# Fused forgetting attention and MoE: the first 128 tokens of all batches as groups of their own, the rest by batch, diagonal blocks in one score chunk

## The chip, the cores and the metric

The kernel runs on one NeuronCore of a Trainium2 chip. The metric is the device time of one execution in microseconds (us), as a median over several runs. In brackets after a ratio stands its 95% interval.

Engines are named as in the profile: PE is TensorE's matmul unit, PEld its weight loads, DVE is VectorE, ACT is ScalarE, POOL is GpSimd, SP is SyncE (here it only issues DMAs).

## The reference

```python
# B=8 batches, H=8 heads, S=576 tokens, D=64;  MoE: d_model 512, d_ff 2048
scores = q @ k.T / sqrt(D)
cum    = cumsum(log(clip(f, 1e-4, 1)), axis=-1)
scores = where(causal, -1e9, scores + cum[q] - cum[k])       # forgetting decay
attn   = softmax(scores);  x = attn @ v                      # (B, H, S, D)
x      = x.transpose(0, 2, 1, 3).reshape(B * S, H * D)       # 4608 x 512
h      = x @ w_in                                            # 4608 x 2048
out    = (h * sigmoid(h)) @ w_out                            # 4608 x 512
```

Attention of one batch feeds 576 rows of the MoE. Attention is small in PE work and heavy on the other engines: in the kernel before, what is not the MoE's takes 61 us of PE's busy time, but 144 us of DVE's and 127 us of ACT's. What is called the MoE here is the two matrix products of `h` and `out`: 1152 matmuls of 128x128 by 512 columns, most of PE's time (282 of 343 us busy in the kernel before). The art of the kernel is to keep PE fed with MoE matmuls while the other engines do the attention of later batches.

## The kernel before

Two heads form a pair `n`, two pairs a quad `m`; a batch has two quads. `scores` makes scaled exponents in chunks of 512 columns and masks the diagonal blocks. A quad's `dn` matmuls make the denominators and the two halves of the numerators. ACT evicts them, DVE takes reciprocals, and `divide` writes the attention output `xT`, which is the MoE's moving operand.

```python
    def scores(n, c):
        # ... matmuls of chunk c into sc; exponent of 2x512 on ACT into u ...
        if c % 2 == 0:
            return
        d = [u[:, :, UO[c - 1] : UO[c - 1] + P], u[:, :, UO[c] : UO[c] + P]]
        for x in d:                                   # four such masks per pair
            nc.vector.tensor_tensor(
                out=x, in0=x, in1=mask[:, None, :].to_broadcast([P, 2, P]), op=ALU.mult
            )
        # ... and mask_t for the last 64 columns if c == 3 ...
```

The MoE is cut into nine groups of 512 tokens. `m1_chunk` makes one 128-row slice of `h` (four W_in matmuls into `hp`, tanh on ACT, one DVE operation into `gt`), `m2_part` a quarter of one output tile (four W_out matmuls into `po`). `fill(n)` emits `n` such units between pieces of attention. The kernel fixes each engine's order itself (`manual_schedule`), and the traces show the operations in the order of emission: in `e1_fill20` below PE waits 1.40 us for a divide while matmuls that need not wait stand behind. `finished` says which groups may be emitted:

```python
    for n in range(2 * NP, NU):                       # the steady part
        b, p = divmod(n, NP)
        scores(n, 0)
        scores(n, 1)
        fill(2)
        if p == 0:
            finished(n - 1)                           # groups of the batch before: only now
        # ... loads, casts, transposes for later pairs ...
        fill(1)
        scores(n, 2)
        scores(n, 3)
        fill(3)
        if n % 2 == 1:
            m = n // 2
            fill(1)
            den(m); rec_part(m, 0)                    # (joined here)
            for e in range(2):
                num(m, e)
            fill(1)
            rec_part(m, 1)
            for e in range(2):
                divide(m, e, nc.gpsimd)
            fill(2)
```

The softmax here doesn't subtract the row's maximum and nothing guards it: scores larger than these inputs give would overflow.

Of the kernel before, what the change touches and what calls it, by code (L numbers as in the profile page):

```python
# [18 lines left out]
def kernel(  # L19
# [14 lines left out]
    NT = B * S  # L34
# [4 lines left out]
    NU = B * NP  # L39
# [3 lines left out]
    NX = 2 * NM + 1  # L43
    NPT = 2 * NP
    NQ = NU // 2
    HD = D // 2
    assert D == 64 and S == 576 and DM == H * D and NP == NCC
# [6 lines left out]
    conv = ctx.enter_context(tc.tile_pool(name="conv", bufs=3))  # L54
    vpool = ctx.enter_context(tc.tile_pool(name="vpool", bufs=3))
# [5 lines left out]
    opool = ctx.enter_context(tc.tile_pool(name="opool", bufs=2))  # L61
# [4 lines left out]


# [6 lines left out]

    def load_qk(n):
        b, p = divmod(n, NP)
        ts = []
        for name, src in (("qf", q), ("kf", k)):
            t = stage.tile([P, 2 * NM * D], FP32, name=name, tag=name, bufs=4)
            for i in range(2):  # L80
                s = src[b, 2 * p + i, 0:SM, :]
                if n < NPT:
                    nc.sync.dma_start(
                        out=t[:, i * NM * D : (i + 1) * NM * D],
                        in_=s.rearrange("(p c) d -> p (c d)", p=P),
                    )
                else:
                    nc.sync.dma_start(
                        out=t[:, :].rearrange("p (c h d) -> p c h d", h=2, d=D)[:, :, i, :],
                        in_=s.rearrange("(c p) d -> p c d", p=P),  # L90
                    )
            ts.append(t)
        qst[n] = tuple(ts)
# [10 lines left out]

    def cast_qk(n, engs):
        b, p = divmod(n, NP)
        t2 = conv.tile([P, NX, 2 * D], BF16, name="qkb", tag="qkb")
        for i, t in enumerate(qst.pop(n)):
            c0 = i * (NM + 1)
            dst = t2[:, c0 : c0 + NM, :]  # L110
            if n < NPT:
                engs[i].tensor_copy(  # L112
                    out=dst.rearrange("p c (h d) -> p c h d", h=2),
                    in_=t[:, :].rearrange("p (h c d) -> p c h d", h=2, d=D),
                )
            else:
                engs[i].tensor_copy(out=dst, in_=t[:, :].rearrange("p (c x) -> p c x", c=NM))  # L117
        nc.gpsimd.tensor_copy(
            out=t2[:, NM, :],
            in_=tst[b][:, 2 * p : 2 * p + 2, :].rearrange("s h d -> s (h d)"),  # L120
        )
        qbf[n] = t2

    def load_v(b, c):
        if b not in vst:
            vst[b] = [
                stage.tile([P, H, D], FP32, name=f"vf{i}", tag=f"vf{i}") for i in range(NM + 1)
            ]
        r = slice(0, P) if c < NM else slice(ST, P)
        nc.sync.dma_start(  # L130
            out=vst[b][c][r, :, :],
            in_=v[b, :, c * P : min(S, (c + 1) * P), :].rearrange("h p d -> p h d"),
        )

    f_sb = setup.tile([BH, S], FP32, name="f_sb")
    nc.sync.dma_start(out=f_sb[:, :], in_=f.rearrange("b h s -> (b h) s"))
    load_qk(0)
    load_tails(0)
    for n in range(1, NP):
        load_qk(n)  # L140
    for c in range(NM + 1):
        load_v(0, c)


    ident_bf = const.tile([P, P], BF16, name="ident_bf")
    make_identity(nc, ident_bf)
    ident_f = const.tile([BH, BH], FP32, name="ident_f")
    make_identity(nc, ident_f)
    mask = const.tile([P, P], BF16, name="mask")
    make_upper_triangular(nc, mask, val=1.0, diag=True)  # L150
    mask_t = const.tile([P, ST], BF16, name="mask_t")
    nc.gpsimd.memset(mask_t[0:ST, :], 0.0)
    make_upper_triangular(nc, mask_t[ST:P, :], val=1.0, diag=True)

    xT = const.tile([P, NCC, NT], BF16, name="xT")
    w_in_bf = const.tile([P, NCC, DFF], BF16, name="w_in_bf")
    w_out_bf = const.tile([P, NFC, DM], BF16, name="w_out_bf")
    w_bf = const.tile([P, NM + 1, BH], BF16, name="w_bf")

# [12 lines left out]
    def load_w_out(i):  # L172
# [5 lines left out]


# [4 lines left out]
    half = setup.tile([BH, 1], FP32, name="half")  # L184
    nc.scalar.activation(out=f_sb[:, :], in_=f_sb[:, :], func=ACT.Ln)
    nc.vector.tensor_tensor_scan(  # L186
        out=cum[:, :],
        data0=f_sb[:, :],
        data1=f_sb[:, :],
        initial=0.0,  # L190
        op0=ALU.add,
        op1=ALU.bypass,
    )
    nc.vector.tensor_scalar_mul(out=half[:, :], in0=cum[:, S - 1 : S], scalar1=0.5)
    wexp = setup.tile([BH, S + ST], FP32, name="wexp")
    nc.scalar.activation(
        out=wexp[:, 0:S], in_=cum[:, :], func=ACT.Exp, bias=half[:, 0:1], scale=-1.0
    )
    cast_qk(0, (nc.vector, nc.vector))
    nc.vector.tensor_copy(out=wexp[:, S : S + ST], in_=wexp[:, SM:S])  # L200

# [7 lines left out]
    qkT: dict[int, bass.AP] = {}  # L209
    us: dict[int, tuple] = {}  # L210

    def convert_v(b, c, eng=nc.gpsimd):
        if b not in vbf:
            vbf[b] = vpool.tile([P, NM + 1, H, D], BF16, name="vp", tag="vp")
        vp = vbf[b]
        r = slice(0, P)
        if c == NM:
            r = slice(ST, P)
            eng.memset(vp[0:ST, NM, :, :], 0.0)
        n = r.stop - r.start  # L220
        eng.tensor_tensor(  # L221
            out=vp[r, c, :, :],
            in0=vst[b][c][r, :, :],
            in1=w_bf[r, c, b * H : (b + 1) * H, None].to_broadcast([n, H, D]),
            op=ALU.mult,
        )


    def k_off(kb):
        return SM if kb == NM else S + ST + kb * P  # L230

    def transposes(n, evac=nc.vector.tensor_copy):
        src = qbf.pop(n)
        t = qktp.tile([P, NX, P], BF16, name="qkT", tag="qkT")
        qkT[n] = t[:, :, :].rearrange("p x c -> p (x c)")
        if n >= NPT:
            nc.sync.dma_start_transpose(
                out=t[:, :, :], in_=src[:, :, :].rearrange("p x c -> p (x c)")
            )
            return  # L240
        for x0 in (0, NM + 1):
            tp = pbig.tile([P, P, NM], FP32, name="tp", tag="big")
            for c in range(NM):
                nc.tensor.matmul(  # L244
                    tp[:, :, c],
                    lhsT=src[:, x0 + c, :],
                    rhs=ident_bf[:, :],
                    start=True,
                    stop=True,
                )  # L250
            evac(  # L251
                out=t[:, x0 : x0 + NM, :].rearrange("p x c -> p (x c)"),
                in_=tp[:, :, :].rearrange("p t c -> p (t c)"),
            )
            if x0 == 0:
                tt = pbig.tile([P, 8 * P], BF16, name="tt", tag="big")
                nc.tensor.transpose(tt[:, 0:P], src[:, NM, :], ident_bf[:, :])
                evac(out=t[:, NM, :], in_=tt[:, 0:P])


    UO = [0]
    for kb in range(NM + 1):
        UO.append(UO[-1] + S - kb * P)
    UW = UO[-1]
    CB = [min(c * 512, UW) for c in range(5)]

    def scores(n, c):
        if c == 0:
            us[n] = upool.tile([P, 2, UW], BF16, name="u", tag="u")
# [3 lines left out]
        c0, c1 = CB[c], CB[c + 1]  # L273
        for kb in range(NM + 1):
            lo, hi = max(UO[kb], c0), min(UO[kb + 1], c1)
            if lo >= hi:
                continue
            q0 = kb * P + lo - UO[kb]
            for i in range(2):
                r = slice(i * D, (i + 1) * D)  # L280
                nc.tensor.matmul(  # L281
                    sc[:, i, lo - c0 : hi - c0],
                    lhsT=t[r, k_off(kb) : k_off(kb) + P],
                    rhs=t[r, q0 : q0 + hi - lo],
                    start=True,
                    stop=True,
                )
# [3 lines left out]
        if c % 2 == 0:  # L291
            return
        d = [u[:, :, UO[c - 1] : UO[c - 1] + P], u[:, :, UO[c] : UO[c] + P]]
        for x in d:
            nc.vector.tensor_tensor(  # L295
                out=x, in0=x, in1=mask[:, None, :].to_broadcast([P, 2, P]), op=ALU.mult
            )
        if c == 3:
            x = u[:, :, UO[NM] : UW]
            nc.vector.tensor_tensor(  # L300
                out=x, in0=x, in1=mask_t[:, None, :].to_broadcast([P, 2, ST]), op=ALU.mult
            )


    QS = 2 * P

    def q_parts(kb):
        if kb * P < QS:
# [284 lines left out]
```

## Time and profile before

| | before |
|---|---|
| time, median | 370.55 us (370.54 to 373.25, 3 runs; 370.98 us with a fourth, which the result below uses) |
| PE busy | 343.0 us, 93% of the span |
| PE's share of the chain that ended last | 73% |
| masks on DVE | 72.7 us in 160 operations |
| MoE alone at the end | from 296 us |

First the page's line of engine totals (busy us, share of the span, instructions), and the rows of PE and of its granted clock, in tenths over 40 equal slices:

```profile
PE 343.0 (93%) x2957; PEld 163.7 (44%) x2957; DVE 240.0 (65%) x368; ACT 233.7 (63%) x363; POOL 141.5 (38%) x195
...
PE   2669778999999999999999999999999999999995
...
PEclk9977996999999999999999999999999999999999
```

Apart from the tail in the last slice, PE loses time only in the first eight slices, 75 us. The busy time by stretches says the same (the columns are length, busy us of each engine with instructions, granted clock, DMA share, GB/s):

```profile
0.00:75.00 75.00, 54.16 (x590) 30.28 (x591) 55.94 (x96) 47.84 (x69) 42.68 (x70) 0.89 1.05 199
75.00:296.00 221.00, 218.28 (x2042) 101.56 (x2041) 159.82 (x240) 158.37 (x248) 96.07 (x124) 1.00 0.68 141
296.00:370.40 74.40, 70.61 (x328) 31.81 (x325) 24.27 (x34) 27.46 (x46) 2.75 (x2) 1.00 0.12 47
```

From 75 us on PE is busy 218 of 221 us at full clock.

```profile
PE hp L381 <- DVE qkT L251: 4.4, 3, 2.5
PE hp L381 <- POOL xT L360: 1.6, 6, 0.7
```

The divides (`POOL xT`) hold up W_in for 1.6 us in the whole run.

### The profile page before, as it was taken

How to read it: one execution, taken by the hardware profiler on the slowest of the kernel's cores; microseconds unless marked ns; L12 is line 12 of the kernel's file. 1: busy time of each engine (PE TensorE's matmuls, PEld its weight loads, DVE VectorE, ACT ScalarE, POOL GpSimd, SP SyncE). 2: the span in 40 equal slices, each digit the busy share in tenths (PEclk: the TensorE clock that was granted, in tenths of full speed). 3: DMA queues.
4: the chain of work that ended last, by engine and by line, in shares of the span. 5: the costliest groups of instructions: out<-in, count | busy, mean ns of one | idle time of the engine just before them, and what ended most of it. 6: DMA issues, size and time to landing. Idle time of an engine off the chain costs nothing.

```text
span 370.4 us, 7558 instructions
## 1 busy us (share of the span) xinstructions
PE 343.0 (93%) x2957; PEld 163.7 (44%) x2957; DVE 240.0 (65%) x368; ACT 233.7 (63%) x363; POOL 141.5 (38%) x195
## 2 busy tenths in 40 slices
PE   2669778999999999999999999999999999999995
PEld 1437342435454545454535454545354544444442
DVE  4678886897667766777777677766776626443400
ACT  4676674876868686868686867686767626344321
POOL 3796582091419150916092609260833020000000
PEclk9977996999999999999999999999999999999999
DMA  6999899999938964796569656976220010001012
GB/s 181 234 192 231 186 190 190 183 196 202 229 77 191 200 135 104 176 213 146 92 144 223 157 104 148 198 159 124 60 62 29 30 58 28 28 30 57 29 58 85
DMA packets 141299, 49.67 MB, mean 134 GB/s; under 512 B 129424, under 2 KB 135568, under 8 KB 141264
## 3 DMA queue, kind: packets, MB, share of 16 engines
q1 hardware_dynamic: 134928, 44.99, 56.7%
q0 software_dynamic: 6336, 4.21, 7.3%
q8 instruction: 23, 0.38, 0.4%
q14 instruction: 12, 0.10, 0.1%
HBM read 36.85 MB, written 9.44 MB: 125 GB/s over the span
## 4 chain that ended last, share of the span: by engine, by line
PE 73%; DVE 11%; ACT 8%; issue 3%; POOL 2%; DMA 1%; POOLq 0%; ACTq 0%
PE hp L381 31%; PE po L408 29%; DVE rec L348 7%; PE dn L331 7%; PE sc L281 6%; ACT u L288 4%; ACT rec L343 3%; POOL xT L360 2%; PE tp L244 1%; DVE qkT L251 1%; ACT th L389 1%; DVE u L295 1%; DVE xT L360 1%; DMA f_sb<-in_f_dram 1%; DVE cum L186 0%
## 5 line engine op out<-in xcount | busy, mean ns | idle before, releaser
L381 PE MATMUL hp<-xT,w_in_bf 128*128 128x512 bf16 x576 | 142.5, 385 | 7.2 <-DVE qkT L251 4.4
L408 PE MATMUL po<-w_out_bf,gt 128*128 128x512 bf16 x576 | 139.7, 380 | 0.0
L390 DVE SCALAR_TENSOR_TENSOR gt<-th,hp 128x512 bf16<-128x512 bf16 x144 | 95.7, 678 | 56.0 <-ACT th L389 55.9
L389 ACT ACTIVATE th<-hp 128x512 bf16<-128x512 f32 x144 | 85.1, 602 | 69.3 <-PE hp L381 69.2
L288 ACT ACTIVATE u<-sc 128x1024 bf16<-128x1024 f32 (+1 forms) x128 | 99.9, 838 | 16.2 <-PE sc L281 16.2
L360 POOL TENSOR_TENSOR xT<-nm,rec 128x576 bf16<-128x576 f32 x28 | 39.3, 1422 | 142.5 <-DVE rec L348 132.1
L295 DVE TENSOR_TENSOR u<-u,mask 128x256 bf16<-128x256 bf16 x128 | 62.9, 518 | 37.3 <-ACT u L288 36.9
L381 PEld LDWEIGHTS <-w_in_bf 128*128 128x128 bf16 x576 | 54.4, 99 | 72.8 <-issue 12.5
L408 PEld LDWEIGHTS <-gt 128*128 128x128 bf16 x576 | 53.4, 98 | 64.5 <-issue 2.5
L348 DVE RECIPROCAL rec<-rec 128x288 f32<-128x288 f32 x32 | 60.2, 1922 | 13.9 <-ACT rec L343 13.9
L221 POOL TENSOR_TENSOR vp<-vf,w_bf 128x512 bf16<-128x512 f32 (+1 forms) x40 | 41.5, 1053 | 2.2 <-DMA vf<-in_v_dram 1.2
L281 PE MATMUL sc<-qkT 64*128 64x64 bf16 (+4 forms) x384 | 34.9, 285 | 4.8 <-ACT u L288 2.9
L417 ACT ACTIVATE osb<-po 128x512 f32<-128x512 f32 x36 | 21.6, 600 | 20.4 <-PE po L408 20.4
L281 PEld LDWEIGHTS <-qkT 64*128 64x128 bf16 x384 | 14.2, 95 | 38.8 <-issue 29.0
L331 PE MATMUL dn<-u,vp 128*32 128x320 bf16 (+4 forms) x896 | 28.7, 270 | 1.7
L355 ACT ACTIVATE nm<-dn 128x576 f32<-128x576 f32 x32 | 20.8, 650 | 6.3 <-PE dn L331 6.0
L331 PEld LDWEIGHTS <-vp 128*32 128x32 bf16 x896 | 22.0, 100 | 6.1 <-issue 3.3
L343 ACT ACTIVATE rec<-dn 128x576 f32<-128x576 f32 x16 | 10.4, 650 | 17.8 <-PE dn L331 17.8
L244 PE MATMUL tp<-ident_bf,qkb 128*128 128x128 bf16 x64 | 11.6, 373 | 6.8 <-DVE qkb L112 6.8
L331 PE MATMUL dn<-u,w_bf 128*32 128x320 bf16 (+4 forms) x448 | 15.1, 272 | 3.0 <-ACT u L288 2.4
L117 POOL CAST qkb<-qf 128x512 bf16<-128x512 f32 x24 | 16.6, 693 | 0.0
L117 POOL CAST qkb<-kf 128x512 bf16<-128x512 f32 x24 | 15.0, 626 | 2.3 <-DMA kf<-in_k_dram 2.3
(42 smaller groups left out, 93.5 us busy)
## 6 DMA issues: line engine op xcount, KB each, us to landing
out_dram<-osb SPq DMA_DIRECT2D x36, 256.0 KB, 2.1
qf<-in_q_dram SPq DMA_DIRECT2D x64, 128.0 KB, 3.2
kf<-in_k_dram SPq DMA_DIRECT2D x64, 128.0 KB, 3.2
vf<-in_v_dram SPq DMA_DIRECT2D x32, 256.0 KB, 4.8
w_in_bf<-in_moe_w_in_dram POOLq DMA_DIRECT2D x8, 256.0 KB, 15.8
w_out_bf<-in_moe_w_out_dram POOLq DMA_DIRECT2D x4, 512.0 KB, 11.7
qktf<-in_q_dram SPq DMA_DIRECT2D x8, 128.0 KB, 3.0
qktf<-in_k_dram SPq DMA_DIRECT2D x8, 128.0 KB, 3.7
```

The costliest lines, as they stand in the source:

```text
L117: engs[i].tensor_copy(out=dst, in_=t[:, :].rearrange("p (c x) -> p c x", c=NM))
L221: eng.tensor_tensor(out=vp[r, c, :, :], in0=vst[b][c][r, :, :], in1=w_bf[r, c, b * H : (b + 1) * H, None].to_broadcast([n, H, D]), op=ALU. ...
L281: nc.tensor.matmul(sc[:, i, lo - c0 : hi - c0], lhsT=t[r, k_off(kb) : k_off(kb) + P], rhs=t[r, q0 : q0 + hi - lo], start=True, stop=True,)
L288: nc.scalar.activation(out=u[:, :, c0:c1], in_=sc[:, :, 0 : c1 - c0], func=ACT.Exp, scale=scale)
L295: nc.vector.tensor_tensor(out=x, in0=x, in1=mask[:, None, :].to_broadcast([P, 2, P]), op=ALU.mult)
L331: nc.tensor.matmul(dn[HD * j : HD * (j + 1), 512 - QS + q0 : 512 - QS + q1], lhsT=w, rhs=u_part(n, i, kb, q0, q1), start=(kb == 0), stop=( ...
L348: nc.vector.reciprocal(out=recs[qd][:, r], in_=recs[qd][:, r])
L360: eng.tensor_tensor(out=xT[:, (2 * qd % NP) + e, b * S : (b + 1) * S], in0=nms.pop((qd, e))[:, :], in1=recs[qd][:, :], op=ALU.mult,)
L381: nc.tensor.matmul(hp[:, :], lhsT=w_in_bf[:, cc, fc * P : (fc + 1) * P], rhs=xT[:, cc, t0 : t0 + TG], start=(cc == 0), stop=(cc == NCC - 1),)
L389: nc.scalar.activation(out=th[:, :], in_=hp[:, :], func=ACT.Tanh, scale=0.5)
L390: nc.vector.scalar_tensor_tensor(out=gt[:, fc, :], in0=th[:, :], scalar=1.0, in1=hp[:, :], op0=ALU.add, op1=ALU.mult,)
L408: nc.tensor.matmul(po[:, :], lhsT=gt[:, fc, tb * P : (tb + 1) * P], rhs=w_out_bf[:, fc, :], start=(fc == 0), stop=(fc == NFC - 1),)
```

## The change

The intent: start the MoE earlier, and give DVE fewer and larger mask operations. The first 128 tokens of a batch need only one diagonal block per head. So these "heads" of all eight batches are attended first, and form three groups (512, 256, 256 tokens). The rest of each batch, 384 tokens, is a group of its own; the last 64 tokens of four batches make a group of 256. In the rest's scores the diagonal blocks lie side by side in one chunk, with one mask. `fill` now takes a budget in microseconds. Cut to its core:

```diff
-    TG = 512
-    NG = NT // TG
+    GW = [4 * P, 2 * P, 2 * P] + [RB] * NM + [NM * ST] + [RB] * (B - NM) + [(B - NM) * ST]
+    # ... load_qk0, turn0 (turning by 64x64 matmuls), scores0, out0: attention of the heads ...
+    CHUNKS = [
+        [(1, 0, P, 0), (2, P, 2 * P, P), (3, 2 * P, RQ, 2 * P), (4, RB, RQ, 2 * P + P + ST)],
+        [(0, 0, RQ, SM)],
+        [(1, P, RQ, SM + RQ), (2, 2 * P, RQ, SM + RQ + 2 * P + ST)],
+    ]
-        for x in d:
-            nc.vector.tensor_tensor(
-                out=x, in0=x, in1=mask[:, None, :].to_broadcast([P, 2, P]), op=ALU.mult
-            )
+        if c == 0:
+            x = u[:, :, 0:SM]
+            nc.vector.tensor_tensor(
+                out=x, in0=x, in1=maskf[:, None, :].to_broadcast([P, 2, SM]), op=ALU.mult
+            )
+    # ... step(): W_in of the next ready group if it is no further on than W_out of the one before
+    FILL = 2.6
+    for m in range(NQ):
+        n = 2 * m
+        scores(n, 0)
+        scores(n, 1)
+        prepare(n)
+        fill(FILL)
+        scores(n, 2)
+        scores(n + 1, 0)
+        prepare(n + 1)
+        fill(FILL)
+        scores(n + 1, 1)
+        scores(n + 1, 2)
+        fill(FILL + 1.0)
+        finish_quad(m)          # dn matmuls, evictions, reciprocals
+        fill(FILL)
+        for e in range(2):
+            divide(m, e, nc.gpsimd)
+        if m % 2 == 1:
+            b = m // 2
+            ready.add(REST_OF[b])       # the batch's own group, at once
+            if b in (NM - 1, B - 1):
+                ready.add(TAILS_OF[b][0])
```

## The prediction

> **What bounds the kernel now.** The tensor engine (PE): 93% busy in the page's engine table, 73% of the chain of work that ended last. By the busy times of stretches, PE is busy 54 of the first 75 us (granted clock 0.89), 218 of 221 us in 75–296 us, and from 296 us does MoE matmuls alone, ending in a tail of some 3 us. In the timeline eight 128x512 matmuls take 1.73 us, 216 ns each[...]. My estimate of PE's work: 1152 MoE matmuls 249 us; attention 9.8 us per batch (scores 0.90 per pair, 2.5 per quad, ten switches at 0.1), 78 us; transposes 8 us: 335 us. About 35 us are lost, nearly 30 before 75 us.
>
> **What the change does** (estimates from those durations).
> - PE work: W_in matmuls become 832 (512, 256, 384 columns)[...]; rest attention 4.35 us per quad, 69 us; heads with their 64x64 turning matmuls 2.3 us per batch, 18 us. Total 337 us: no less than before.
> - Start: MoE can begin once four heads are done. DVE paces this: per batch an eviction 0.6, a mask 0.6–0.9, a reciprocal of 256 (6.4 ns per element) 1.65, a divide 0.65 us, after some 11 us (f, log, scan, exponent). First MoE matmul at 27 us (before: 36.5), then dense, with some 6 us of stalls where batches 4, 5 meet group 1. The rest starts at 80 us with 24 us lost.
> - DVE: 128 masks of 256 (518 ns mean) and 32 of 128 become 40 of 1024, saving about 35 us, off the critical path. ACT: 32 small exponents fewer, 64 more W_in evictions, about +10 us.
>
> **Where it loses.** Groups follow batches. A batch's rest gives 384 tokens x 54 ns = 20.8 us of MoE; two quads ask for 22.8. By the instruction order, no MoE work is left at the ends of quads 1, 3, 5 and 7: after the dn matmuls come ten score matmuls and then W_in matmuls of the group just attended, which wait for an evict 0.5, two reciprocals 2.95 and POOL divides about 2.5 us. PE idles nearly 4 us, four times: 15 us. The work also separates into quads with only W_in and quads with only W_out matmuls; the first load ACT to about 95%. The end of the last quad waits 2 us. After quad 8 groups overlap again and PE should be dense.
>
> **Sum.** 337 work + 24 start + 15 starvation + 2 last quad + 3 tail = 381; less 2 for doubt about the small matmuls' costs: 379 us. 8 in 10: 364 to 392 us. Chances: faster by over 2% 0.12, within 2% 0.40, slower 0.48.
>
> **What would show each step.** First hp matmul at 25–30 us, rest scores from 75–85 us; four waits of hp for POOL's divide, 3–4 us each, some 33 us apart, between 105 and 215 us; hp of 384 columns in runs of six chunks; the mask group at 0.7–0.9 us x40; dense PE afterwards; the MoE-only end about 33 us rather than 74.
>
> **What would make it wrong.** Divides landing sooner than their chain suggests, so no starvation (then about 363). A start sooner than 27 us. Weights landing late (second W_in half after 34 us), which would stall the early MoE and add 5–10 us. [...] ACT, not PE, limiting the W_in-only quads.

The sum came to 381 us, 379 us after the 2 us for doubt. The 0.6 us for 256 additional W_in matmuls is contained in the 337 us of work (249 + 69 + 18 = 336 without it). The 6.4 ns per element can be read from DVE's timeline of the kernel before: two reciprocals of 288 elements start at 106.10 us, and the next operation at 109.78, 3.68 us later.

## More of the kernel before

A verdict is "unclear" when the interval reaches over the mark of 2%.

From the groups of instructions (busy us, mean ns of one, idle before), the two kinds of MoE matmul and the masks, and from the list of waits (total us, times, longest) what W_in matmuls waited for:

```profile
L381 PE MATMUL hp<-xT,w_in_bf 128*128 128x512 bf16 x576 | 142.5, 385 | 7.2 <-DVE qkT L251 4.4
L408 PE MATMUL po<-w_out_bf,gt 128*128 128x512 bf16 x576 | 139.7, 380 | 0.0
...
L295 DVE TENSOR_TENSOR u<-u,mask 128x256 bf16<-128x256 bf16 x128 | 62.9, 518 | 37.3 <-ACT u L288 36.9
```

## The result, and the profile after

The changed kernel takes 404.25 us (403.94 to 404.49, 4 runs) against 370.98 us (370.54 to 373.25). The ratio is 1.087, with a 95% interval of 1.0832 to 1.0908. A ratio here is worked out by the program that took the times, over the runs of the same rounds, so it is not quite the ratio of the medians. The span of the profiled run is 402.4 us, 32.0 us more than before.

The same views as before. The engine totals, with the rows of PE and of the clock:

```profile
PE 349.2 (87%) x3682; PEld 192.7 (48%) x3717; DVE 208.6 (52%) x310; ACT 235.7 (59%) x408; POOL 151.7 (38%) x252
...
PE   3639799899879959996995999999799989979995
...
PEclk9958999999969999996999899999899989999999
```

The holes are no longer at the start alone: there is one about every 3.5 slices, and the clock dips next to most of them. The busy time by stretches (columns as before):

```profile
0.00:80.00 80.00, 58.64 (x718) 35.98 (x725) 50.98 (x71) 34.84 (x58) 38.75 (x69) 0.91 0.94 166
80.00:359.00 279.00, 252.00 (x2748) 134.94 (x2771) 142.07 (x207) 183.57 (x313) 112.95 (x183) 0.95 0.55 118
359.00:402.40 43.40, 38.51 (x221) 21.73 (x223) 15.53 (x32) 17.31 (x39) 0.00 (x0) 0.99 0.13 43
```

In the middle stretch PE is idle 27 of 279 us and has a mean clock of 0.95. The groups, and the waits of W_in:

```profile
L504 PE MATMUL po<-w_out_bf,gt 128*128 128x512 bf16 x544 | 135.1, 381 | 3.0 <-issue 1.0 <-ACT osb L513 0.6 <-PE dn L429 0.2
L478 PE MATMUL hp<-x,w_in_bf 128*128 128x384 bf16 x512 | 105.7, 350 | 21.6 <-POOL x L460 20.5 <-DVE gt L487 0.8
...
L410 DVE TENSOR_TENSOR u<-u,maskf 128x1024 bf16<-128x1024 bf16 x32 | 27.1, 846 | 36.5 <-ACT u L405 36.4
```

```profile
PE hp L478 <- POOL x L460: 20.5, 14, 2.7
PE hp L478 <- DVE x L321: 4.9, 2, 4.0
PE hp L478 <- DVE gt L487: 3.5, 4, 2.5
```

The masks of the rest take 27.1 us, and those of the heads 6.9 us more, where all masks took 72.7 us before. The wait of W_in for the divides rose from 1.6 to 20.5 us. (The counts of matmuls are a little short, as some records are missing from a trace.) One such wait in PE's timeline, at the end of quad 1 (start, us, line, operation, count, and in brackets the idle time before it):

```profile
107.03 0.61 PE L429 MATMUL dn<-u,vp 128*32 128x128 bf16 x24
108.10 0.40 PE L398 MATMUL sc<-qkT 64*128 64x128 bf16 x8 [0.46 <-ACT nm L447]
108.54 0.37 PE L398 MATMUL sc<-qkT,kT 64*128 64x448 bf16 x2
108.84 0.50 PE L478 MATMUL hp<-x,w_in_bf 128*128 128x384 bf16 x2
112.06 0.48 PE L478 MATMUL hp<-x,w_in_bf 128*128 128x384 bf16 x1 [2.72 <-POOL x L460]
113.29 4.32 PE L478 MATMUL hp<-x,w_in_bf 128*128 128x384 bf16 x13 [0.75 <-POOL x L460]
117.54 1.04 PE L398 MATMUL sc<-qkT 64*128 64x320 bf16 x12
```

After the last `dn` matmuls come the next quad's scores and then at once W_in matmuls of the group that was attended just before. The first two read the parts of `x` that quad 0 had written; the third waits for quad 1's divides. Then 13 matmuls of 384 columns take 4.32 us, where 16 take 2.77 us elsewhere. The chain they waited for, in DVE's and POOL's timelines of the same time:

```profile
107.65 2.97 DVE L452 RECIPROCAL rec<-rec 128x224 f32<-128x224 f32 x2 [4.16 <-ACT rec L444]
```

```profile
110.79 2.73 POOL L460 TENSOR_TENSOR x<-nm,rec 128x384 bf16<-128x384 f32 x4 [3.66 <-DVE rec L452]
```

The divides end at 113.5 us, 5.9 us after the last `dn` matmul.

The waits in PE's timeline are at the ends of quads 1, 3, 5, 7, 11, 13 and 15: 3.93, 4.14, 3.98, 4.15, 2.32, 2.03 and 2.26 us of idle time (scores' waits included), 22.8 us together. The clock is at half (granted 0.5, and 1.0 elsewhere) in six stretches after 110 us, one from near the end of each of these but the last: two of 6.8 and four of 3.4 us, 27.3 us in all. PE was busy 24.4 us of that, so an estimate of what the half clock cost is 24.4 / 2 = 12.2 us. Idle time and clock together are 35 us, a little more than the whole 32.0 us of difference. In the 3.4 us before each of the six stretches, PE's records cover 0.3 to 1.4 us.

### The profile page after: what moved, and what is told of

Same layout as the page of the kernel before. It is cut to its first block, busy times and chain, and to the rows that moved or that the text cites. A ratio compares the mean times of both kernels' runs of the same rounds, so it can differ in the third digit from the quotient of the medians.

```text
span 402.4 us, 9181 instructions
## 1 busy us (share of the span) xinstructions
PE 349.2 (87%) x3682; PEld 192.7 (48%) x3717; DVE 208.6 (52%) x310; ACT 235.7 (59%) x408; POOL 151.7 (38%) x252
## 4 chain that ended last, share of the span: by engine, by line
PE 67%; DVE 9%; issue 6%; ACT 6%; DMA 5%; POOL 4%; SPq 2%; POOLq 0%; ACTq 0%
PE po L504 28%; PE hp L478 27%; PE dn L429 6%; PE sc L398 5%; DMA vf<-in_v_dram 4%; DVE rec L452 4%; POOL x L460 3%; ACT u L405 2%; DVE gt L487 2%; DVE rec L317 2%; ACT th L486 1%; ACT rec L444 1%; DMA w_in_bf<-in_moe_w_in_dram 1%; SPq L127 1%; DVE x L321 1%
## 5 line engine op out<-in xcount | busy, mean ns | idle before, releaser
L478 PE MATMUL hp<-x,w_in_bf 128*128 128x384 bf16 (+2 forms) x829 | 156.2, 332 | 30.3 <-POOL x L460 20.5
L487 DVE SCALAR_TENSOR_TENSOR gt<-th,hp 128x384 bf16<-128x384 bf16 (+2 forms) x208 | 103.0, 518 | 87.2 <-ACT th L486 84.9
L486 ACT ACTIVATE th<-hp 128x384 bf16<-128x384 f32 (+2 forms) x208 | 94.6, 473 | 80.7 <-PE hp L478 74.9
L478 PEld LDWEIGHTS <-w_in_bf 128*128 128x128 bf16 x832 | 81.9, 102 | 96.3 <-issue 52.9
L460 POOL TENSOR_TENSOR x<-nm,rec 128x384 bf16<-128x384 f32 x64 | 46.3, 754 | 171.8 <-DVE rec L452 171.8
L452 DVE RECIPROCAL rec<-rec 128x224 f32<-128x224 f32 x32 | 47.4, 1524 | 38.5 <-ACT rec L444 38.5
L410 DVE TENSOR_TENSOR u<-u,maskf 128x1024 bf16<-128x1024 bf16 x32 | 27.1, 846 | 36.5 <-ACT u L405 36.4
L398 PE MATMUL sc<-qkT 64*128 64x128 bf16 (+3 forms) x384 | 23.2, 242 | 2.0 <-ACT nm L447 2.0
L429 PE MATMUL dn<-u,vp 128*32 128x128 bf16 (+3 forms) x768 | 19.7, 237 | 0.0
L335 POOL CAST qkb<-qf 128x384 bf16<-128x384 f32 x32 | 18.4, 574 | 0.8 <-PE hp L478 0.5
```

The source lines that it names most:

```text
L335: nc.gpsimd.tensor_copy(out=t2[:, c0 : c0 + NR, :].rearrange("p c x -> p (c x)"), in_=t[:, :, :, :].rearrange("p c h d -> p (c h d)"),)
L398: nc.tensor.matmul(sc[:, i, o - c0 : o - c0 + q1 - q0], lhsT=kt, rhs=t[r, q0:q1], start=True, stop=True,)
L410: nc.vector.tensor_tensor(out=x, in0=x, in1=maskf[:, None, :].to_broadcast([P, 2, SM]), op=ALU.mult)
L429: nc.tensor.matmul(dn[HD * j : HD * (j + 1), q0:q1], lhsT=w, rhs=us[n][:, i, o : o + q1 - q0], start=(kb == 0), stop=(kb == NM),)
L452: nc.vector.reciprocal(out=recs[qd][:, r], in_=recs[qd][:, r])
L460: eng.tensor_tensor(out=xg(g)[:, cc, g0 : g0 + c1 - c0], in0=nm[:, c0:c1], in1=rec[:, c0:c1], op=ALU.mult,)
```

## The experiments

Theory 1: PE starves at the batch ends. By the order of emission it has no other MoE work there, waits for the divides, and then runs at half clock. Theory 2: PE simply has more to do (832 W_in matmuls for 576, turning matmuls, narrower pieces). Theory 3: ACT limits the new mix.

### Less MoE work asked for: `e1_fill20`

```diff
-    FILL = 2.6
+    FILL = 2.0
```

> One number changed: the MoE budget between attention pieces is 2.0 instead of 2.6 us, so that by the order of emission no quad runs out of MoE work. Theory 1 (the matrix engine starves at batch ends because two quads ask for more MoE work than one batch's rest supplies, waits for the divides, and then runs at half clock): the waits of hp for POOL's divide fall from 20 us to under 4, the half-clock stretches after 110 us vanish, and the time falls by 28 to 36 us to 368-376 us. Theory 2 (the matrix engine simply has more work: 832 instead of 576 W_in matmuls, turning matmuls, narrower attention pieces): waits move elsewhere and the time stays above 392 us. Theory 3 (ScalarE limits the new mix): shorter gaps between attention pieces load it more, so 400 us or more.

Measured: 384.22 us (381.85 to 386.5), ratio 1.0328 [1.0277, 1.0379]. That refutes theories 2 and 3 as the main cause: one number that removes no work takes 20 us away. But it misses my range by 8 us. The waits of W_in for the divides, from the list of waits, and the end of quad 1 in PE's timeline:

```profile
PE hp L478 <- POOL x L460: 10.5, 8, 1.5
```

```profile
104.50 1.67 PE L504 MATMUL po<-w_out_bf,gt 128*128 128x512 bf16 x7 [0.16 <-issue]
106.10 0.40 PE L398 MATMUL sc<-qkT 64*128 64x128 bf16 x8
106.34 0.35 PE L398 MATMUL sc<-qkT,kT 64*128 64x448 bf16 x2
106.62 0.50 PE L478 MATMUL hp<-x,w_in_bf 128*128 128x384 bf16 x2
108.52 0.32 PE L478 MATMUL hp<-x,w_in_bf 128*128 128x384 bf16 x1 [1.40 <-POOL x L460]
110.20 2.65 PE L478 MATMUL hp<-x,w_in_bf 128*128 128x384 bf16 x9 [1.35 <-POOL x L460]
```

W_out work was now left at the batch end. PE did 1.7 us of it, and still waited, because the rule that picks the next unit took W_in of the fresh group before the rest of W_out. By the order of emission 1, 4, 7 and 10 units of W_out stood behind it at the ends of quads 1, 3, 5 and 7. So "no work left" was not quite the cause. What counts is how much other work stands in PE's queue between a batch's attention and the first W_in matmul of its own group. I call this theory 1a.

### The clock by itself: `e2_warm`

```diff
+    def warm(n):                       # result never read
+        jk = pbig.tile([P, 512], FP32, name="jk", tag="big")
+        for _ in range(n):
+            nc.tensor.matmul(jk[:, :], lhsT=w_in_bf[:, 0, 0:P], rhs=w_in_bf[:, 0, 0:512], start=True, stop=True)
     ...
         prepare(n)
+        if m in (2, 4, 6, 8):
+            warm(16)
+        if m in (12, 14):
+            warm(10)
         fill(FILL)
```

> The changed kernel with its budget of 2.6 us, but with matmuls whose result nobody reads (16 of 128x512, 3.45 us, at the first MoE slot of quads 2, 4, 6, 8, and 10 of them, 2.15 us, at quads 12 and 14) filling the time in which the matrix engine would wait for the divides. No work is taken away and no wait is shortened. If the half clock after each wait is a cost of its own (theory 1, second half): the granted clock stays at 1.0 after 110 us and the time falls by 9 to 13 us, to 391-395 us. If the clock dips are only a record of idleness: 402-406 us.

Measured: 394.55 us, ratio 1.0613 [1.0589, 1.0637], 9.7 us less than the changed kernel by the medians and about as much by the two ratios (1.0613 for 1.087). The busy time by stretches (columns as before) shows a mean clock of 1.00, and PE's timeline shows the dummy matmuls (`jk`) in place of the wait and 13 W_in matmuls at full rate, 2.27 us in place of 4.32:

```profile
80.00:380.00 300.00, 288.53 (x3017) 158.44 (x3048) 156.97 (x239) 198.62 (x347) 112.90 (x183) 1.00 0.54 113
```

```profile
109.75 3.40 PE L676 MATMUL jk<-w_in_bf 128*128 128x512 bf16 x15 [0.16 <-issue]
112.99 0.65 PE L478 MATMUL hp<-x,w_in_bf 128*128 128x384 bf16 x3
113.98 2.27 PE L478 MATMUL hp<-x,w_in_bf 128*128 128x384 bf16 x13 [0.34 <-POOL x L460]
```

More work made the kernel faster. The half clock is a cost of its own, some 10 us of the 33.

### The length of the chain: `e6_divdve`

```diff
         for e in range(2):
-            divide(m, e, nc.gpsimd)
+            divide(m, e, nc.gpsimd if e == 0 else nc.vector)
```

> The changed kernel (budget 2.6, early release) with the second of each quad's two divides on VectorE instead of GpSimd, so that the two run side by side and the chain from attention to W_in is some 1.0 to 1.3 us shorter. Theory 1: each of the seven waits shrinks by about 1 us, some half-clock stretches vanish with it: 390 to 398 us. If the waits are only due to missing work and not to the length of the chain, or if VectorE's own queue eats the gain: 402 to 406 us.

Measured: 393.34 us, ratio 1.0578 [1.0515, 1.064]. W_in's wait for POOL's divides is 14.7 us in the list of waits, for 20.5. The half-clock stretches after 110 us shrank from 27.3 to 17.1 us. Shortening the chain by about 1 us at a time gave 11 us in all: 5.8 us less of waiting, and some 4 us by the same estimate for the half clock (16.1 us busy at half clock for 24.4). So the waits do follow the chain.

### Releasing the group later: `e4_late18a`, `e5_late18b`

```diff
-    FILL = 2.6
+    FILL = 1.8
+    def finished(b):
+        ready.add(REST_OF[b])
+        if b in (NM - 1, B - 1):
+            ready.add(TAILS_OF[b][0])
     ...
         fill(FILL)
+        if m > 0 and m % 2 == 0:        # e4: here; e5: after the second fill(FILL)
+            finished(m // 2 - 1)
         scores(n, 2)
     ...
-        if m % 2 == 1:
-            b = m // 2
-            ready.add(REST_OF[b])
-            if b in (NM - 1, B - 1):
-                ready.add(TAILS_OF[b][0])
+        if m == NQ - 1:
+            finished(m // 2)
```

> Budget 1.8 us, and a batch's rest group is released to the MoE only after the first MoE slot of the next quad (it was: right after its divides are issued). By the emission order no slot is empty, and 3.9 to 4.3 us of other MoE work stands between the end of a batch's attention and the first W_in matmul of its own group in the four early batches (the first run: 1.7 us; the change: 0). The divides land some 4.5 us after the attention ends, so the waits should almost close. Theory 1a (what counts is how much other work is queued ahead of a fresh group on the in-order matrix engine): hp's waits for POOL's divide under 3 us in total, no half clock after 110 us, 368 to 373 us. If the 384 us of the first run came from other costs: 380 us or more.

> As the run before it, but the group is released after the second MoE slot: 5.2 to 5.4 us of other work ahead of it in the early batches, with one slot about 1 us short at quad 2. Theory 1a: no wait for POOL's divide at all, 367 to 373 us, within 2 us of the other. If later release starves the engine instead: 3 us or more slower than the other.

Measured: 372.81 us (ratio 1.0022 [0.9961, 1.0083]) and 372.55 us (ratio 1.0022 [0.9957, 1.0087]). Both expectations of theory 1a are met, and W_in's wait for POOL's divides is all but gone from both lists of waits. The same place in PE's timeline of the first of the two:

```profile
102.30 0.62 PE L429 MATMUL dn<-u,vp 128*32 128x128 bf16 x24
102.84 2.76 PE L504 MATMUL po<-w_out_bf,gt 128*128 128x512 bf16 x12
105.54 0.40 PE L398 MATMUL sc<-qkT 64*128 64x128 bf16 x8
105.77 0.35 PE L398 MATMUL sc<-qkT,kT 64*128 64x448 bf16 x2
106.06 1.90 PE L504 MATMUL po<-w_out_bf,gt 128*128 128x512 bf16 x8
107.89 0.62 PE L398 MATMUL sc<-qkT 64*128 64x320 bf16 x12
108.44 1.47 PE L478 MATMUL hp<-x,w_in_bf 128*128 128x384 bf16 x8
```

Twenty W_out matmuls and the scores now stand between the `dn` matmuls and W_in, 5.5 us. The last divide that W_in reads ends at 108.73 us, just before the fourth W_in matmul, which reads it first, starts at 108.94. No half-clock stretch is left in this run from 33 us to the end of the matmuls; the second run has one, of 3.4 us at 49 us, still in the start. So 31 of the 33 us (some 30 by the repeat `e4_again` below) come from the budget and the order of release, two scheduling choices around an otherwise unchanged set of operations.

No run separates the two. Followed through from the code of `step` and `fill`, budget 1.8 with the early release would leave 1.7 to 2.6 us of other MoE work between attention and W_in at the ends of quads 1, 3 and 5; the late release makes that 3.9 to 4.3 us. From quad 7 on, the smaller budget alone leaves 6.7 us and more, because it puts MoE work off. So the release should matter at the first three batch ends only, but that is worked out and not measured.

### The masks: `e3_mask2`, `e10_mask2late`, `e7_diag`

The first two apply the mask of the rest's diagonal chunk twice (the values are 0 and 1, so the result is the same):

```diff
                 out=x, in0=x, in1=maskf[:, None, :].to_broadcast([P, 2, SM]), op=ALU.mult
             )
+            nc.vector.tensor_tensor(
+                out=x, in0=x, in1=maskf[:, None, :].to_broadcast([P, 2, SM]), op=ALU.mult
+            )
```

> Budget 2.0 as in the first run, and the mask of the diagonal chunk applied twice (0 and 1, so the result is the same): VectorE gets 32 more operations of about 0.85 us, 27 us in all, which is most of what the single score chunk saved it. If VectorE is off the critical path, as I predicted: within 2 us of the run with budget 2.0. If the diagonal chunk's saving counts: 8 us or more slower than that run.

> The late-release version with every mask of the rest applied twice: 27 us more of VectorE, as in the third run, but now on a kernel whose matrix engine has no waits for divides. The third run cost 6.5 us where such waits were left. If VectorE mattered there only as part of the chain that the waits follow: under 2 us slower than the base. If VectorE limits the W_in stretches by itself: 5 us or more slower.

`e3_mask2` took 390.69 us, 6.5 us more than the run with budget 2.0. It had four half-clock stretches after 80 us where the other had two. That lies between the two outcomes written down (within 2 us, or 8 us and more). It also waited 4.2 us for W_in's first half at the start, but its base had waited about as long for DVE there, so this explains little of the 6.5 us. `e10_mask2late` took 379.99 us, ratio 1.022 [1.0166, 1.0274], unclear at the mark of 2%; its base, run again on the same chip as `e4_again`, took 374.28 us, ratio 1.0068 [1.0001, 1.0135].

> The late-release version with budget 1.8 again, on the chip of the next three, as their base: 371 to 374 us, ratio to before 1.000 to 1.006.

The base's median was 0.3 us above the range that I gave for it. So in the repaired kernel 25.7 us more of masks cost 5.7 us. That is the second of the outcomes written down (5 us or more): DVE is not free there, and the prediction's "off the critical path" does not hold for it. W_in's waits for DVE to give its PSUM buffers back, in the run with doubled masks and in its base:

```profile
PE hp L481 <- DVE gt L490: 6.9, 9, 2.5
PE hp L478 <- DVE gt L487: 4.9, 6, 2.5
```

These are 2.0 us of the 5.7. W_out's wait for the same operation rose by 1.1 us; the rest is spread over small waits and is not explained here.

The opposite case, the kernel before with the single mask alone:

```diff
+    CHUNKS = [
+        [(kb, kb * P, kb * P + P, kb * P) for kb in range(NM)],
+        [(0, P, S, SM), (3, SM, S, SM + S - P)],
+        [(1, 2 * P, S, 2 * SM), (2, 3 * P, S, 2 * SM + S - 2 * P)],
+        [(NM, SM, S, 3 * SM)],
+    ]
-        d = [u[:, :, UO[c - 1] : UO[c - 1] + P], u[:, :, UO[c] : UO[c] + P]]
-        for x in d:      # four masks of 128x256
+        if c == 0:       # one of 128x1024
```

> The kernel before, with one part of the change alone: the four diagonal blocks lie in one score chunk with one mask operation of 128x1024 in place of four of 128x256. The off-diagonal pieces fill the other chunks, so that the exponents keep their sizes; attention needs 10 instead of 7 pieces per head and sum (120 for 84 matmuls). VectorE's masks fall by some 25 to 35 us. I expect no gain, as VectorE isn't on the critical path: 0 to 8 us slower than before for the additional small matmuls. If the masks were on the path: 3 us or more faster.

Measured: 376.13 us, ratio 1.0152 [1.0061, 1.0244], unclear at the mark of 2% (one of the four runs, 380.36 us, was slow; the median of the others is 376.05). DVE's busy time fell from 240.0 to 211.5 us, and the kernel got no faster, but some 4.5 us slower. The run also adds matmuls (120 for 84 in a quad's sums), so by itself it can't exclude that they ate a gain. The trace of the kernel before speaks against a large one: in the whole run PE waited 0.6 us for masks and 0.9 us for `gt`. So there I take the masks to be off the critical path.

### The start: `e8_warmstart`, `e9_actevict`, `e11_win`

These build on the late release, to see what bounds what is left. First dummy matmuls in the two waits just ahead of the first W_in matmul, then also both evictions of turned heads on ACT, then also W_in's second half issued earlier:

```diff
# e8
     out0(2)
+    warm(8)
     out0(3)
+    warm(16)
     ready.add(0)
# e9 = e8 and
-            ((qT0[b], nc.scalar.copy), (kT0[b], nc.vector.tensor_copy))
+            ((qT0[b], nc.scalar.copy), (kT0[b], nc.scalar.copy))
# e11 = e9 and
     convert_v0(1)
+    load_w_in(1)
     out0(0)
     ...
     load_qk0(5)
-    load_w_in(1)
```

> The late-release version (budget 1.8) with 8 and 16 matmuls whose result nobody reads in the two waits of the matrix engine just before its first W_in matmul (2.4 and 4.0 us long there), and nothing else. If the half clock of 22 to 33 us comes from those waits, it vanishes and the first 40 W_in matmuls take 8.7 instead of 11.3 us: 2 to 3 us faster than the base. If the half clock there was set by the sparse work before, nothing changes.

> As the run before it, and the turned keys of the heads are also evicted by ScalarE, not VectorE (8 times 0.69 us), since VectorE's queue paces the heads. If VectorE sets the start: first W_in matmul about 2 us earlier (25.5 instead of 27.6 us), and 3 to 5 us faster than the base, about 368 us, which would be some 1% faster than the kernel before. If ScalarE's two evictions in a row hold up the scores instead: no faster than the run before it.

> As the run with ScalarE's evictions, and the second half of W_in is fetched 9 us earlier: issued after the second batch's heads are converted, ahead of the heads of batches 4 and 5 (it was behind them). In the run before, the matrix engine waited 3.24 us for this half at 38 us, which ate the earlier start. If that wait is all that stands between: no wait for W_in, and 3 us faster than that run, some 369 to 371 us and 0.2 to 1% faster than the kernel before. If something else takes over (heads of batches 4 and 5 landing later, the values of batch 3): no faster than 373 us.

`e8_warmstart`: 372.88 us, ratio 1.0052 [0.9989, 1.0114], where its base had 1.0068. The clock did rise, from 0.95 to 1.00 in 28–80 us, and the first 40 W_in matmuls took 9.2 us in the two lines of the timeline that hold them (7.55 and 1.68 us, with a 0.4 us wait between), for 11.07 us in the base. But the gain in time, 1.4 us by the medians where 2 to 3 were expected, is within the intervals: inconclusive.

`e9_actevict`: 373.74 us, ratio 1.0052 [0.9996, 1.0108], no faster. The first W_in matmul came at 27.8 us and not at 25.5, so the expectation for a start set by DVE was missed. And after 32 W_in matmuls at full clock PE waited, because the second half of W_in had not landed:

```profile
27.79 7.07 PE L478 MATMUL hp<-x,w_in_bf 128*128 128x512 bf16 x32 [0.61 <-DVE x L321]
38.10 1.90 PE L478 MATMUL hp<-x,w_in_bf 128*128 128x512 bf16 x8 [3.24 <-DMA w_in_bf<-in_moe_w_in_dram]
```

`e11_win`: 371.3 us (370.68 to 372.62), ratio 0.9995 [0.9966, 1.0025]. That wait is gone from PE's list. The median is 2.4 us less than in the run before it (on another chip), just above the 369 to 371 us expected, and the ratio lies within the range of 0.2 to 1% faster only at the edge of its interval. This is the best version that I found, and it equals the kernel before. I found none that beats both.

## Why the prediction was right or wrong

- Forecast as slower by over 2% with the highest chance, 0.48, and it was slower: 8.7%. The time of 379 us, and its range up to 392, were too low.
- What bounds the kernel before, and PE's work of the two: the version without the waits takes 372.8 us against the 364 us that my terms give without starvation (337 + 24 + 3). Some 9 us were not in the sum. PE was busy 338.6 us in `e4_late18a`, close to the 337, so most of the 9 us is waiting; I have not split it further. The claim that the change brings PE no less work fits, though no run tests it alone: without its waits the changed kernel ties with the kernel before.
- The start was right: first W_in matmul at 27.6 us (predicted 27), first scores of the rest at 80.3 us (predicted 80). The end with MoE alone was not: at least 43 us, from 359 us on, for some 33.
- The waits at quads 1, 3, 5 and 7 were right in place and in size: 4 us each, predicted nearly 4, "PE idles nearly 4 us, four times: 15 us".
- The term that was mis-sized is "15 starvation + 2 last quad". It measured 22.8 us of idle time and an estimated 12.2 us of half clock, 35 us for 17; that is 18 of the 25 us by which the sum was too low. Two things were missing. First, "After quad 8 groups overlap again and PE should be dense" failed: quads 11 and 13 waited as well, 2.0 to 2.3 us each. There MoE work was left, but the emission order put the fresh group's W_in right behind the scores. Secondly, I costed an idle microsecond as one microsecond and left the clock out. `e2_warm` shows that the half clock after the waits took 9.7 us of its own.
- My cause, work running out, was only half of it. `e1_fill20` left work over and kept waits of half the size. `e4_late18a` and `e5_late18b`, which also release the group later, removed them. (They changed the budget from 2.0 to 1.8 as well; budget 1.8 with the early release and the late release at another budget were not run.)
- "Saving about 35 us, off the critical path" fits the kernel before (0.6 us of waits for masks; `e7_diag`: 28.5 us less DVE time, no gain). For the changed kernel, once its waits are gone, it was wrong: 25.7 us more masks cost 5.7 us in `e10_mask2late`.
- ACT limiting the W_in-only quads, which I gave as a risk, is not seen as a large cost (ACT's busy time rose by 2.0 us, and not by about 10): two DVE waits of 0.41 us are all that PE's timeline shows in the W_in runs of quads 2, 4, 6 and 8.

## What to carry to other kernels

On an engine that executes in the order of emission, as PE does here (in `e1_fill20` it waits 1.40 us for a divide with other matmuls behind), count how much other work stands between the producer of a fresh group and its first consumer, and hold the group back, or keep other work in hand, until that distance is longer than the chain between them (here 5.9 us from the last `dn` matmul to the end of the divides); "there is work left" is not enough. Group sizes that follow the data (a batch, a group) make this easy to get wrong, because the group becomes ready just when the last one is used up. When PE idles for microseconds in a row, cost the half clock after it too (here 27.3 us of it, at six waits of 2.0 to 4.2 us); if the wait can't be removed, dummy matmuls in it can pay. They gave 9.7 us of 404 in `e2_warm`; at the start, in `e8_warmstart`, the clock rose from 0.95 to 1.00 as well, but the time did not clearly fall.
